# First token chunk as plain rows transposed on the matmul engine, loads reordered over two queues, gate logits in two parts

## The chip, the cores and the metric

The kernel runs on one core of one Trainium2 chip. The metric is device time in microseconds (us) of a whole execution. The profiler's span is about 1.5 us shorter than the timed run (293.3 against 294.8 us before the change).

Engine names in the profile: PE is the matmul engine, PEld its weight loads, DVE the vector engine, ACT the scalar engine, POOL the GpSimd engine, SP the sync engine. SPq and ACTq are the instruction streams of SP and ACT in so far as they issue DMA. "Full clock" and "half clock" are the clock that PE was granted, 1.00 and 0.50 in the tables. "The page" is the profile's summary page.

## The reference

One block of 2048 tokens, width 512, in bf16. Two branches are mixed by a per-token gate:

```python
g = sigmoid((x * gate_w).sum(-1))
# A: 4 segments of 512 tokens, 32 heads of 16; phi(t) = t + 1 where t > 0, else exp(t)
q, k, v = x @ wq, x @ wk, x @ wv
for s in range(4):
    a_dot = softmax(q_s k_s^T * scale + mask) v_s
    a_mem = phi(q_s) M / (phi(q_s) z + 1e-6)      # memory of earlier segments
    o_s   = sigmoid(beta) * a_mem + (1 - sigmoid(beta)) * a_dot
    M, z  = M + phi(k_s)^T v_s, z + sum(phi(k_s))
a = concat(o) @ wo
# B: feed-forward
b = (relu(x @ W_gate) * (x @ W_up)) @ W_down      # hidden width 1792
out = g * a + (1 - g) * b
```

A chunk of x is the 512 tokens of one segment: segment 0 needs only the first 512 tokens; the gate needs all tokens, but segment 0 only its own.

## The kernel before

The Python program is a list scheduler. It gives every operation an estimated duration, runs a model of the engines at build time, and emits one fixed instruction order for each engine, with semaphore waits between engines. So each engine runs in order: if the next instruction waits, all behind it wait. The model's DMA part is crude:

```python
# Sched.place(), for a DMA (cut): arrival times that the fixed order is built on
issued = start + occ
self.dma_free[e] = max(self.dma_free[e], issued) + op.nbytes / 150.0
op.end = self.dma_free[e] + 1500.0
```

Loads. x is wanted with features on partitions (`xT`), so it is loaded by 16 transposing DMAs on SP (4 for each chunk of 512 tokens), while ACT issues all weights:

```python
wload("wq", ...); wload("wk", ...)            # ACT queue; 512 KB each
...                                           # gate_w, beta, wv, gate/up weights, wo, wd: 7.6 MB in all
for c in range(NSEG):
    for kt in range(KT):
        xl.append(dma("sp", lambda e, c=c, kt=kt: e.dma_start_transpose(V.xT[:, kt, c * 512:(c + 1) * 512], A_x[...]),
                      1 << 17, occ=1280.0, writes=[f"xT{c}_{kt}"], name=f"ldx{c}_{kt}"))
```

PE is kept busy at the start with twelve matmuls on zeros (`warm`). The gate's logits are one group of 64 small matmuls that reads all of `xT` (`gmm`).

The keys for the memory update go through SP as well. ACT computes `ek = exp(k)`, DVE turns it into `phi(k)` in place, and SP transposes it into `phik`.

```python
acts.append(act(... V.ek[:, G, :] = exp(V.kT[:, G, :]) ..., writes=[f"ek{G}"], name=f"kexp{s}_{G}"))
sbs.append(dve(... V.ek[:, G, :] = min(V.ek, ttmp) ...,      writes=[f"ek{G}"], name=f"kphi{s}_{G}"))
sps.append(dma("sp", lambda e, G=G: e.dma_start_transpose(V.phik[:, :, G * 128:(G + 1) * 128], V.ek[:, G, :]), ...,
               reads=[f"ek{G}"], writes=[f"phik{G}"], name=f"kT2{s}_{G}"))
# memory update of segment s, first half: reads phik0, phik1
pes.append(pe(fn, mm(160, 8), reads=[f"phik{2 * hf}", f"phik{2 * hf + 1}"] + va(s), name=f"mu{s}_{hf}", ...))
```

Note two users of a key transpose: the memory update (`mu`) reads its result, and the *next* segment's `kexp` overwrites its source `ek`, so it must wait until the transpose has read it.

The softmax here doesn't subtract the row's maximum and nothing guards it: scores larger than these inputs give would overflow.

## Time and profile before

| | before |
|---|---|
| time, median of 3 | 294.81 us (294.5 to 295.98) |
| span of the profiled run | 293.3 us |
| PE busy | 269.9 us, 92% |
| first projection matmul | 17.81 us |
| first and last exponential of attention | 31.61 and 259.72 us |

PE is the bound. Its line on the page (busy us, share of the span, instructions):

```profile
PE 269.9 (92%) x2136; PEld 115.0 (39%) x2172; DVE 198.7 (68%) x391; ACT 184.2 (63%) x142; POOL 93.4 (32%) x150
...
```

Every matmul has one weight load, so 2136 matmuls against 2172 weight loads says that 36 matmul records are missing. A missing record can show as a gap of 0.16 to 0.24 us put down to "issue".

The table of windows (stretch in us, then its length, then busy us and instruction count of each engine; then the granted clock of PE, the mean busy share of the DMA engines, and GB/s):

```profile
core 0: us, PE busy (x) PEld busy (x) DVE busy (x) ACT busy (x) POOL busy (x), PEclk, DMA share, GB/s
0.00:5.00 5.00, 3.75 (x9) 1.34 (x10) 2.27 (x6) 0.00 (x0) 2.96 (x13) 1.00 0.61 155
5.00:10.00 5.00, 1.55 (x4) 0.30 (x2) 0.00 (x0) 0.00 (x0) 0.00 (x0) 1.00 1.03 137
10.00:20.00 10.00, 2.19 (x6) 0.84 (x7) 0.28 (x1) 1.09 (x1) 0.00 (x0) 0.50 1.10 336
20.00:35.00 15.00, 14.80 (x69) 5.96 (x69) 12.65 (x32) 6.34 (x10) 0.73 (x1) 0.88 1.17 310
35.00:40.00 5.00, 4.14 (x74) 2.37 (x74) 4.89 (x13) 4.18 (x4) 1.63 (x3) 1.00 0.55 79
40.00:50.00 10.00, 9.76 (x68) 4.26 (x67) 8.28 (x23) 7.55 (x9) 3.38 (x5) 0.83 0.19 39
```

The DMA engines are full from 5 to 35 us, but at 5 to 10 us they move only 137 GB/s. PE does nearly nothing until 18 us. The waits of the first 60 us say why (the engine, the tile and line that waited, what ended the wait; then us in all, times, longest), and the timeline shows the first real matmul:

```profile
PE psA L522 <- DMA xT<-in_A_x_dram: 11.3, 1, 11.3
```

```profile
1.25 5.30 PE L468 MATMUL psL<-rl 128*128 128x512 bf16 x12 [1.25 <-DVE rl L460]
...
17.81 1.87 PE L522 MATMUL psA<-xT,wq 128*128 128x512 bf16 x4 [11.26 <-DMA xT<-in_A_x_dram]
...
38.63 1.74 PE L486 MATMUL psA<-gwc,xT 128*128 128x1 bf16 x64 [0.70 <-DVE kp L538]
...
42.22 1.91 PE L522 MATMUL psA<-xT,wq 128*128 128x512 bf16 x4
```

The first two columns are start and length; the bracket is idle time of that engine just before, and what ended it. Line 522 is the projections; line 486 the gate. Wq was there at about 4.9 us; x came at 17.8. Four projection matmuls took 1.91 us at 42.22 us, and four such take 1.03 us elsewhere. After the gate PE ran at half clock for 3.4 us (40.77 to 44.18 us by the clock records of the trace).

### The profile page before, as it was taken

Reading aid. Unit: us, or ns where it says so; the run is one execution under the profiler, and the core shown is the slowest. Engines: PE = TensorE matmul, PEld = TensorE weight load, DVE = VectorE, ACT = ScalarE, POOL = GpSimd, SP = SyncE. Lnnn points to the kernel's source line nnn. Section 1 sums busy time; section 2 is a strip of 40 time slices with the busy share of each in tenths; the row PEclk is TensorE's granted clock in tenths of the full one; section 3 lists DMA queues with packets and bytes.
Section 4 is the critical chain, followed back from the end, with each engine's and each line's share of the span. In section 5 each row is a group of like instructions: output and inputs, shape, how many; then the busy total and the mean of one; then the engine's idle time right before and its main releaser. Section 6 shows DMA issues by size and latency. Waiting matters only on the chain.

```text
span 293.3 us, 5236 instructions
## 1 busy us (share of the span) xinstructions
PE 269.9 (92%) x2136; PEld 115.0 (39%) x2172; DVE 198.7 (68%) x391; ACT 184.2 (63%) x142; POOL 93.4 (32%) x150
## 2 busy tenths in 40 slices
PE   7059989799999999999999999999999999999895
PEld 2024344334444444434344434344344343344342
DVE  3027998999899989377889986458866354867100
ACT  0023678679785977768857967777677776763111
POOL 4000142553442533442424343343234334330000
PEclk9658979999999999999999999999999999999999
DMA  8999920001004131200001100100020000000011
GB/s 172 217 368 325 245 58 16 2 9 29 2 19 68 26 47 27 38 18 20 0 2 36 38 1 20 36 20 0 2 54 20 18 33 23 2 0 1 2 36 36
DMA packets 30791, 15.29 MB, mean 52 GB/s; under 512 B 22832, under 2 KB 30768, under 8 KB 30768
## 3 DMA queue, kind: packets, MB, share of 16 engines
q1 hardware_dynamic: 24064, 7.35, 12.9%
q10 hardware_dynamic: 6704, 7.61, 8.5%
q8 instruction: 17, 0.28, 0.4%
q14 instruction: 6, 0.05, 0.1%
HBM read 7.61 MB, written 2.10 MB: 33 GB/s over the span
## 4 chain that ended last, share of the span: by engine, by line
PE 85%; DVE 6%; DMA 4%; issue 2%; SPq 1%; ACT 0%; DVEq 0%; ACTq 0%
PE psA L685 32%; PE psA L716 17%; PE psA L522 10%; PE psL L615 8%; PE psA L640 6%; PE psA L708 5%; DMA xT<-in_A_x_dram 4%; PE psA L520 4%; SPq L437 1%; DVE vaug L546 1%; DVE kp L538 1%; PE psA L561 1%; PE psA L590 1%; DVE gexpT L494 1%; DVE qT L529 1%
## 5 line engine op out<-in xcount | busy, mean ns | idle before, releaser
L620 ACT ACTIVATE E<-psL 128x2048 bf16<-128x2048 f32 x80 | 150.1, 1876 | 44.3 <-PE psL L615 43.8
L623 POOL TENSOR_SCALAR_AFFINE_SELECT E<-E 128x512 bf16<-128x512 bf16 x128 | 83.9, 673 | 167.3 <-ACT E L620 166.1
L685 PE MATMUL psA<-xT,wg 128*128 128x512 bf16 x216 | 58.9, 380 | 1.8 <-DVE Tn L645 0.8
L685 PE MATMUL psA<-xT,wu 128*128 128x512 bf16 x217 | 57.3, 379 | 1.0 <-issue 1.0
L716 PE MATMUL psA<-wd,hT 128*128 128x512 bf16 x216 | 52.6, 380 | 0.8 <-issue 0.5
L696 DVE TENSOR_TENSOR hT<-psA,rl 128x512 bf16<-128x512 f32 x56 | 38.0, 679 | 8.3 <-PE psA L685 7.9
L645 DVE STREAM_TRANSPOSE Tn<-psA 128x512 f32<-128x512 f32 x32 | 21.5, 698 | 17.6 <-PE psA L640 17.4
L615 PE MATMUL psL<-qT,kp 32*128 32x384 bf16 (+3 forms) x512 | 31.7, 301 | 0.9 <-ACT E L620 0.8
L685 PEld LDWEIGHTS psA<-xT,wu 128*128 128x128 bf16 x224 | 20.9, 98 | 25.2 <-issue 1.4
L716 PEld LDWEIGHTS psA<-wd,hT 128*128 128x128 bf16 x224 | 20.4, 98 | 25.1 <-issue 3.4
L685 PEld LDWEIGHTS psA<-xT,wg 128*128 128x128 bf16 x224 | 19.6, 98 | 26.1 <-issue 4.3
L522 PE MATMUL psA<-xT,wq 128*128 128x512 bf16 x58 | 18.1, 432 | 11.8 <-DMA xT<-in_A_x_dram 11.3
L693 ACT ACTIVATE rl<-psA 128x512 bf16<-128x512 f32 x25 | 14.9, 596 | 16.8 <-PE psA L685 16.8
L529 DVE CAST qT<-psA 128x512 bf16<-128x512 f32 x16 | 11.0, 688 | 19.4 <-PE psA L522 19.3
L694 DVE TENSOR_SCALAR rl<-psA 128x512 bf16<-128x512 f32 x31 | 21.1, 682 | 4.1 <-PE psA L685 3.6
L615 PEld LDWEIGHTS psL<-qT,kp 32*128 32x128 bf16 x512 | 8.9, 92 | 32.5 <-ACT E L620 21.6
L640 PE MATMUL psA<-E,vaug 128*17 128x256 bf16 (+3 forms) x512 | 21.1, 300 | 0.0
L522 PE MATMUL psA<-xT,wk 128*128 128x512 bf16 x62 | 18.6, 418 | 0.3 <-issue 0.2
L721 ACT ACTIVATE osb<-psA,omg 128x512 bf16<-128x512 f32 x10 | 6.9, 687 | 17.3 <-PE psA L716 17.3
L708 PE MATMUL psA<-wo,oT 128*128 128x512 bf16 x62 | 16.2, 380 | 1.2 <-DVE hT L696 0.9
L520 PE MATMUL psA<-wv,xT 128*128 128x512 bf16 x61 | 15.0, 380 | 0.3 <-issue 0.2
L640 PEld LDWEIGHTS psA<-E,vaug 128*17 128x17 bf16 x512 | 10.5, 90 | 11.2 <-issue 4.2
(61 smaller groups left out, 201.7 us busy)
## 6 DMA issues: line engine op xcount, KB each, us to landing
out_dram<-osb SPq DMA_DIRECT2D x16, 128.0 KB, 1.7
wg<-in_B_W_gate_dram ACTq DMA_DIRECT2D x2, 896.0 KB, 14.1
wu<-in_B_W_up_dram ACTq DMA_DIRECT2D x2, 896.0 KB, 15.6
wd<-in_B_W_down_dram ACTq DMA_DIRECT2D x1, 1792.0 KB, 18.0
wq<-in_A_wq_dram ACTq DMA_DIRECT2D x1, 512.0 KB, 4.1
wk<-in_A_wk_dram ACTq DMA_DIRECT2D x1, 512.0 KB, 8.1
wv<-in_A_wv_dram ACTq DMA_DIRECT2D x1, 512.0 KB, 10.5
wo<-in_A_wo_dram ACTq DMA_DIRECT2D x1, 512.0 KB, 17.0
```

The costliest lines, as they stand in the source:

```text
L520: ins = e.matmul(A(ep)[:, :], lhsT=V.xT[:, kt, tok + col * 128:tok + (col + 1) * 128], rhs=w[:, kt, :], start=(kt == 0), stop=(kt == KT - 1))
L522: ins = e.matmul(A(ep)[:, :], lhsT=w[:, kt, col * 128:(col + 1) * 128], rhs=V.xT[:, kt, tok:tok + 512], start=(kt == 0), stop=(kt == KT - 1))
L615: ins = q.matmul(PL[:, jj, o:o + w], lhsT=V.kp[32 * jj:32 * jj + 32, kslot(s, n), 128 * j:128 * j + 128], rhs=V.qT[32 * jj:32 * jj + 32, q ...
L620: acts.append(act(lambda a, e=e: a.activation(V.E[:, e, :, :], PL[:, :, :], ACT.Exp, scale=SCALE), t_act(2048), reads=[f"bankL{b}" for b i ...
L623: pools.append(pool(lambda g, ap=ap: g.affine_select(out=ap, in_=ap, compare_op=ALU.is_ge, fill=0.0, base=0, pattern=[[0, 4], [1, 128]], c ...
L640: ins = q.matmul(A(ep)[32 * jj:32 * jj + 17, c:512], lhsT=V.vaug[:, s % 2, j, 8 * G + 2 * jj + p, :], rhs=V.E[:, e, jj, o:o + w], start=(j ...
L645: ds.append(dve(lambda e, p=p, ep=eps[p]: e.transpose(V.Tn[:, p, :], A(ep)[:, :]), t_dve(512), writes=[f"Tn{p}"], name=f"tr{s}_{G}_{p}", e ...
L685: ins = e.matmul(A(ep)[:, :], lhsT=w[:, kt, f * 128:(f + 1) * 128], rhs=V.xT[:, kt, c * 512:(c + 1) * 512], start=(kt == 0), stop=(kt == K ...
L694: ("dve", lambda e, ep=eg, r=r: e.tensor_scalar(V.rl[:, r, :], A(ep)[:, :], 0.0, None, ALU.max), t_dve(512))],
L696: evs.append(dve(lambda e, ep=eu, r=r, hs=hs: e.tensor_tensor(V.hT[:, hs, :], A(ep)[:, :], V.rl[:, r, :], ALU.mult), t_dve(512), reads=[f" ...
L708: ins = e.matmul(A(ep)[:, :], lhsT=V.oT[:, o0 + G, i * 128:(i + 1) * 128], rhs=V.wo[:, G, :], start=(G == 0), stop=False)
L716: ins = e.matmul(A(ep)[:, :], lhsT=V.hT[:, slots[f], i * 128:(i + 1) * 128], rhs=V.wd[:, f, :], start=False, stop=(f == NF - 1))
```

## The change

The intent is to start earlier. The first chunk comes as plain rows (4 x 128 KB, split over SP and ACT) into a part of `hT` that is not in use yet; 16 matmuls with an identity transpose it into PSUM, and four copies put it into `xT`. wq, wk, wv follow in halves on both queues; all later loads are on SP in order of first use, with the x of chunks 2 and 3 last. The gate is split into a part for chunk 0 and a part for the rest. The cost model of the scheduler changes too (one shared DMA rate of 330 bytes/ns and 1800 ns to land).

```diff
-            self.dma_free[e] = max(self.dma_free[e], issued) + op.nbytes / 150.0
-            op.end = self.dma_free[e] + 1500.0
+            self.dma_busy = max(self.dma_busy, issued) + op.nbytes / 330.0
+            op.end = self.dma_busy + 1800.0
...
+    for i, eng in enumerate(("sp", "act", "sp", "act")):
+        load(eng, [f"hT{i}"], V.hT[:, i, :], x0[:, i, :], 1 << 17)
+    for nm, w, src in (("wq", V.wq, A_wq), ("wk", V.wk, A_wk), ("wv", V.wv, A_wv)):
+        load("sp", [nm + "a"], w[:, 0:2, :], r[:, 0:2, :], 1 << 18)
+        load("act", [nm + "b"], w[:, 2:4, :], r[:, 2:4, :], 1 << 18)
+    load("sp", ["braw"], ...)          # beta
+    load_gu(0)                         # first half of gate and up weights
+    lsp.append(... ld_gw ...)          # gate_w
+    load_x(1)                          # 4 transposing loads
+    load_gu(1)
+    load("sp", ["wo"], ...)
+    load("sp", ["wd"], ...)
+    for c in range(2, NSEG):
+        load_x(c)                      # 8 transposing loads
...
-        for i in range(12):            # warm-up matmuls
+    xps, xcs = [warm(WARM, 0)], []     # WARM = 5
+    for i in range(4):
+        def fx(e, i=i):
+            for kt in range(KT):
+                ins = e.matmul(PL[:, i, kt * 128:(kt + 1) * 128], lhsT=V.hT[:, i, kt * 128:(kt + 1) * 128], rhs=V.ident[:], start=True, stop=True)
...
-    gp = pe(f_gmm, NT * KT * 30.0, reads=[x for c in range(NSEG) for x in xt(c)] + ["gwc"], name="gmm", ep=ep_g, role="w")
+    for part, (t0, t1) in enumerate(((0, 4), (4, NT))):
+        gq["pe"].append(pe(f_gmm, (t1 - t0) * KT * 26.0, reads=[x for c in range(t0 // 4, t1 // 4) for x in xt(c)] + ["gwc"], name=f"gmm{part}", ...))
...
-  "oa{s}_{i}" reads [f"hT{x}" for x in slots]
+  "oa{s}_{i}" reads [f"hT{x}" for x in (slots if s < NSEG - 1 else slots[:NF - 4])]
```

Cuts are marked by "..."; left out are the small gate copies (now on DVE or ACT) and a few duration estimates.

More of the change, by code (lines that the diff above doesn't have):

```diff
@@ L16 @@
 SWITCH = 100.0
+WARM = 5
 def mm(n, k=1):
@@ L95, in __init__ @@
         self.res = {}
-        self.now = {e: 0.0 for e in self.ENGS}
+        self.now = {e: 800.0 for e in self.ENGS}
         self.mode = "f"
@@ L100, in __init__ @@
         self.dma_end = {}
-        self.dma_free = {e: 0.0 for e in self.ENGS}
+        self.dma_busy = 0.0
         self.prog = {e: [] for e in self.ENGS}
@@ L353, in plan @@
         ("gexp", [128, NT], F32), ("omg", [128, NT], F32), ("gexpT", [128, NT * 4], F32), ("c2g", [128, NT, 32], F32),
-        ("rden", [128, 32], F32), ("rdg", [128, 32], F32), ("rdm", [128, 128], F32), ("pm8", [128, 8], F32), ("pm", [128, 2], F32),
+        ("rden", [128, 32], F32), ("rdg", [128, 32], F32), ("rdm", [128, 128], F32), ("pm8", [128, 8], F32), ("pm", [128, 2], F32), ("ident", [128, 128], BF16),
     ]
@@ L407, in xt, with load, load_gu, load_x @@
         return [f"xT{c}_{kt}" for kt in range(KT)]
-    loads = []
-    def wload(name, dst, src, nbytes):
-        loads.append(dma("act", lambda e, dst=dst, src=src: e.dma_start(dst, src), nbytes, writes=[name], name="ld" + name))
-    wload("wq", V.wq[:], A_wq.rearrange("(kt p) n -> p kt n", p=128), 1 << 19)
-    wload("wk", V.wk[:], A_wk.rearrange("(kt p) n -> p kt n", p=128), 1 << 19)
-    with nc.allow_non_contiguous_dma(reason="one column of gate weights"):
-        gsrc = gate_w.rearrange("(kt p) -> p kt", p=128)
+    lact, lsp = [], []
+    def load(eng, names, dst, src, nbytes, occ=460.0):
+        (lact if eng == "act" else lsp).append(dma(eng, lambda e, dst=dst, src=src: e.dma_start(dst, src), nbytes, occ=occ, writes=names, name="ld" + names[0]))
+    x0 = A_x[0, 0:512, :].rearrange("(i p) d -> p i d", p=128)
+    for i, eng in enumerate(("sp", "act", "sp", "act")):
+        load(eng, [f"hT{i}"], V.hT[:, i, :], x0[:, i, :], 1 << 17)
+    for nm, w, src in (("wq", V.wq, A_wq), ("wk", V.wk, A_wk), ("wv", V.wv, A_wv)):
+        r = src.rearrange("(kt p) n -> p kt n", p=128)
+        load("sp", [nm + "a"], w[:, 0:2, :], r[:, 0:2, :], 1 << 18)
+        load("act", [nm + "b"], w[:, 2:4, :], r[:, 2:4, :], 1 << 18)
+    wgr = W_g.rearrange("(kt p) n -> p kt n", p=128)
+    wur = W_u.rearrange("(kt p) n -> p kt n", p=128)
+    half = (NF // 2) * 128
+    hs_ = ((0, half), (half, NF * 128))
+    def load_gu(h):
+        a, b = hs_[h]
+        load("sp", [f"wg{h}"], V.wg[:, :, a:b], wgr[:, :, a:b], 512 * 2 * (b - a))
+        load("sp", [f"wu{h}"], V.wu[:, :, a:b], wur[:, :, a:b], 512 * 2 * (b - a))
+    def load_x(c):
+        for kt in range(KT):
+            lsp.append(dma("sp", lambda e, c=c, kt=kt: e.dma_start_transpose(V.xT[:, kt, c * 512:(c + 1) * 512], A_x[0, c * 512:(c + 1) * 512, kt * 128:(kt + 1) * 128]),
+                           1 << 17, occ=1280.0, writes=[f"xT{c}_{kt}"], name=f"ldx{c}_{kt}"))
+    load("sp", ["braw"], V.braw[:], A_beta.partition_broadcast(128), 8192)
+    load_gu(0)
+    gsrc = gate_w.rearrange("(kt p) -> p kt", p=128)
     def ld_gw(e):
@@ L420, in ld_gw @@
             return e.dma_start(V.gwc[:], gsrc)
-    loads.append(dma("act", ld_gw, 60000, writes=["gwc"], name="ldgw"))
-    wload("braw", V.braw[:], A_beta.partition_broadcast(128), 8192)
-    wload("wv", V.wv[:], A_wv.rearrange("(kt p) n -> p kt n", p=128), 1 << 19)
-    wgr = W_g.rearrange("(kt p) n -> p kt n", p=128)
-    wur = W_u.rearrange("(kt p) n -> p kt n", p=128)
-    half = (NF // 2) * 128
-    for h, (a, b) in enumerate(((0, half), (half, NF * 128))):
-        wload(f"wg{h}", V.wg[:, :, a:b], wgr[:, :, a:b], 512 * 2 * (b - a))
-        wload(f"wu{h}", V.wu[:, :, a:b], wur[:, :, a:b], 512 * 2 * (b - a))
-    wload("wo", V.wo[:], A_wo.rearrange("(g p) n -> p g n", p=128), 1 << 19)
-    wload("wd", V.wd[:], W_d.rearrange("(f p) n -> p f n", p=128), NF * 128 * 1024)
-    sc.queue(0, loads)
-    xl = []
-    for c in range(NSEG):
-        for kt in range(KT):
-            xl.append(dma("sp", lambda e, c=c, kt=kt: e.dma_start_transpose(V.xT[:, kt, c * 512:(c + 1) * 512], A_x[0, c * 512:(c + 1) * 512, kt * 128:(kt + 1) * 128]),
-                          1 << 17, occ=1280.0, writes=[f"xT{c}_{kt}"], name=f"ldx{c}_{kt}"))
-    sc.queue(0, xl)
+    lsp.append(dma("sp", ld_gw, 60000, writes=["gwc"], name="ldgw"))
+    load_x(1)
+    load_gu(1)
+    load("sp", ["wo"], V.wo[:], A_wo.rearrange("(g p) n -> p g n", p=128), 1 << 19)
+    load("sp", ["wd"], V.wd[:], W_d.rearrange("(f p) n -> p f n", p=128), NF * 128 * 1024)
+    for c in range(2, NSEG):
+        load_x(c)
+    sc.queue(0, lact)
+    sc.queue(0, lsp)
     st = []
+    st.append(pool(lambda e: e.memset(V.ident[:], 1.0), 150, writes=["ident"], name="id0"))
+    st.append(pool(lambda e: e.affine_select(out=V.ident[:], in_=V.ident[:], compare_op=ALU.is_equal, fill=0.0, base=0, pattern=[[1, 128]], channel_multiplier=-1),
+                   260, reads=["ident"], writes=["ident"], name="id1"))
     st.append(pool(lambda e: e.memset(V.pm8[:], 1.0), 150, writes=["pm8"], name="pm8a"))
@@ L464, in program, with warm, fn @@
     sc.queue(0, ds)
-    def f_warm(e):
-        for i in range(12):
-            ins = e.matmul(PL[:, 0, :], lhsT=V.rl[:, 0, 0:128], rhs=V.rl[:, 0, :], start=True, stop=True)
-        return ins
-    sc.queue(0, [pe(f_warm, 5000, reads=["rl0"], writes=["bankL0"], name="warm")])
+    def warm(n, k):
+        def fn(e):
+            for i in range(n):
+                ins = e.matmul(PA[0][:, :], lhsT=V.rl[:, 0, 0:128], rhs=V.rl[:, 0, :], start=True, stop=True)
+            return ins
+        return pe(fn, n * 427, reads=["rl0"], writes=["init0"], name=f"warm{k}")
+    xps, xcs = [warm(WARM, 0)], []
+    for i in range(4):
+        def fx(e, i=i):
+            for kt in range(KT):
+                ins = e.matmul(PL[:, i, kt * 128:(kt + 1) * 128], lhsT=V.hT[:, i, kt * 128:(kt + 1) * 128], rhs=V.ident[:], start=True, stop=True)
+            return ins
+        xps.append(pe(fx, 430, reads=[f"hT{i}", "ident"], writes=[f"bankL{i}"], name=f"xt{i}"))
+        dst = V.xT[:, :, i * 128:(i + 1) * 128]
+        srcp = PL[:, i, :].rearrange("q (k t) -> q k t", k=KT)
+        xcs.append(sc.add(Op([("dve", lambda e, d=dst, s_=srcp: e.tensor_copy(d, s_), t_dve(512)),
+                              ("act", lambda e, d=dst, s_=srcp: e.activation(d, s_, ACT.Copy), t_act(512))],
+                             reads=[f"bankL{i}"], writes=[f"xT0_{i}"], name=f"xc{i}")))
+    sc.queue(0, xps)
+    sc.queue(0, xcs)
     cst = [act(lambda e: e.activation(V.eb[:], V.braw[:], ACT.Exp), 300, reads=["braw"], writes=["eb"], name="eb")]
@@ L479, in program @@
     sc.queue(1, [t for t in cst if t.eng == "dve"])
-    ep_g = Epoch()
-    def f_gmm(e):
-        for t in range(NT):
-            for kt in range(KT):
-                ins = e.matmul(A(ep_g)[:, t:t + 1], lhsT=V.xT[:, kt, t * 128:(t + 1) * 128], rhs=V.gwc[:, kt:kt + 1], start=(kt == 0), stop=(kt == KT - 1))
-        return ins
-    gp = pe(f_gmm, NT * KT * 30.0, reads=[x for c in range(NSEG) for x in xt(c)] + ["gwc"], name="gmm", ep=ep_g, role="w")
-    ga = act(lambda e: e.activation(V.gexp[:, :], A(ep_g)[:, 0:NT], ACT.Exp), 190, writes=["gexp"], name="gexp", ep=ep_g, role="r")
@@ L490, in program @@
-    gd = [dve(lambda e: e.tensor_scalar(V.omg[:], V.gexp[:], 1.0, None, ALU.add), 180, reads=["gexp"], writes=["omg1"], name="omg1"),
-          dve(lambda e: e.reciprocal(V.omg[:], V.omg[:]), 250, reads=["omg1"], writes=["omg"], name="omg")]
-    for a in range(4):
-        for jj in range(4):
-            gd.append(dve(lambda e, a=a, jj=jj: e.tensor_copy(V.gexpT[32 * jj:32 * jj + 32, :].rearrange("q (t a) -> q t a", a=4)[:, :, a], V.gexp[32 * a:32 * a + 32, :]),
-                          150, reads=["gexp"], writes=[f"gexpT{a}{jj}"], name="gexpT"))
@@ L496, in program, with f_gmm @@
-    gd.append(dve(lambda e: e.tensor_tensor(V.c2g[:], V.eb[:, :].unsqueeze(1).to_broadcast([128, NT, 32]), V.gexp[:, :].unsqueeze(2).to_broadcast([128, NT, 32]), ALU.mult),
-                  t_dve(NT * 32), reads=["eb", "gexp"], writes=["c2g"], name="c2g"))
-    gexpT_r = [f"gexpT{a}{jj}" for a in range(4) for jj in range(4)]
-    sc.queue(3, [gp])
-    sc.queue(1, [ga])
-    sc.queue(1, gd)
+    gexpT_r = {}
+    gq = {"pe": [], "act": [], "dve": [], "flex": []}
+    for part, (t0, t1) in enumerate(((0, 4), (4, NT))):
+        ep_g = Epoch()
+        def f_gmm(e, t0=t0, t1=t1, ep_g=ep_g):
+            for t in range(t0, t1):
+                for kt in range(KT):
+                    ins = e.matmul(A(ep_g)[:, t - t0:t - t0 + 1], lhsT=V.xT[:, kt, t * 128:(t + 1) * 128], rhs=V.gwc[:, kt:kt + 1], start=(kt == 0), stop=(kt == KT - 1))
+            return ins
+        gq["pe"].append(pe(f_gmm, (t1 - t0) * KT * 26.0, reads=[x for c in range(t0 // 4, t1 // 4) for x in xt(c)] + ["gwc"], name=f"gmm{part}", ep=ep_g, role="w"))
+        gx = V.gexp[:, t0:t1]
+        gq["act"].append(act(lambda e, t0=t0, t1=t1, gx=gx, ep_g=ep_g: e.activation(gx, A(ep_g)[:, 0:t1 - t0], ACT.Exp), 190, writes=[f"gexp{part}"], name="gexp", ep=ep_g, role="r"))
+        om = V.omg[:, t0:t1]
+        gq["dve"].append(dve(lambda e, om=om, gx=gx: e.tensor_scalar(om, gx, 1.0, None, ALU.add), 180, reads=[f"gexp{part}"], writes=[f"omg1{part}"], name="omg1"))
+        gq["dve"].append(dve(lambda e, om=om: e.reciprocal(om, om), 250, reads=[f"omg1{part}"], writes=[f"omg{part}"], name="omg"))
+        gexpT_r[part] = []
+        for a in range(4):
+            for jj in range(4):
+                dst = V.gexpT[32 * jj:32 * jj + 32, :].rearrange("q (t a) -> q t a", a=4)[:, t0:t1, a]
+                gq["flex"].append(sc.add(Op([("dve", lambda e, a=a, dst=dst, t0=t0, t1=t1: e.tensor_copy(dst, V.gexp[32 * a:32 * a + 32, t0:t1]), 150),
+                                             ("act", lambda e, a=a, dst=dst, t0=t0, t1=t1: e.activation(dst, V.gexp[32 * a:32 * a + 32, t0:t1], ACT.Copy), 215)],
+                                            reads=[f"gexp{part}"], writes=[f"gexpT{part}_{a}{jj}"], name="gexpT")))
+                gexpT_r[part].append(f"gexpT{part}_{a}{jj}")
+        if part:
+            gq["dve"].append(dve(lambda e, t0=t0: e.tensor_tensor(V.c2g[:, t0:, :], V.eb[:, :].unsqueeze(1).to_broadcast([128, NT - t0, 32]), V.gexp[:, t0:].unsqueeze(2).to_broadcast([128, NT - t0, 32]), ALU.mult),
+                                 t_dve((NT - t0) * 32), reads=["eb", f"gexp{part}"], writes=["c2g"], name="c2g"))
@@ L503, in kslot @@
+    sc.queue(2, gq["pe"][:1])
+    sc.queue(4, gq["pe"][1:])
+    sc.queue(1, gq["act"])
+    sc.queue(1, gq["dve"])
+    sc.queue(2, gq["flex"])
     def kslot(s, n):
@@ L523, in fn @@
                     return ins
-                pes.append(pe(fn, mm(512, 2), reads=[wname] + xt(s), name=f"{name}{s}_{col}", ep=ep, role="w2" if k0 else "w"))
+                pes.append(pe(fn, mm(512, 2), reads=[wname + ("b" if k0 else "a")] + xt(s), name=f"{name}{s}_{col}", ep=ep, role="w2" if k0 else "w"))
             return ep
@@ L537, in proj @@
                 ks = kslot(s, 2 * G + p)
-                evs.append(dve(lambda e, G=G, p=p, ks=ks: e.tensor_scalar(V.kp[:, ks, :], V.kT[:, G, :], V.pm[:, p:p + 1], None, ALU.mult), t_dve(512, 4), reads=[f"kT{G}", "pm"], writes=[f"kp{ks}"], name=f"kmask{s}_{G}_{p}"))
+                evs.append(dve(lambda e, G=G, p=p, ks=ks: e.tensor_scalar(V.kp[:, ks, :], V.kT[:, G, :], V.pm[:, p:p + 1], None, ALU.mult), 417, reads=[f"kT{G}", "pm"], writes=[f"kp{ks}"], name=f"kmask{s}_{G}_{p}"))
             if s < NSEG - 1:
@@ L649, in flush @@
             ds.append(dve(lambda e: e.reciprocal(rv, Tv[:, :, :, 16]), 345, reads=["Tn0", "Tn1"], writes=["rden"], name=f"rden{s}_{G}"))
-            ds.append(dve(lambda e: e.tensor_tensor(gv, rv, V.gexpT[:, 16 * s:16 * s + 16].unsqueeze(1).to_broadcast([128, 2, 16]), ALU.mult), 180, reads=["rden"] + gexpT_r, writes=["rdg"], name=f"rdg{s}_{G}"))
+            ds.append(dve(lambda e: e.tensor_tensor(gv, rv, V.gexpT[:, 16 * s:16 * s + 16].unsqueeze(1).to_broadcast([128, 2, 16]), ALU.mult), 264, reads=["rden"] + gexpT_r[min(s, 1)], writes=["rdg"], name=f"rdg{s}_{G}"))
             av = V.adT[:, :].rearrange("q (c p e) -> q p c e", p=2, e=16)
-            ds.append(dve(lambda e: e.tensor_tensor(av, Tv[:, :, :, 0:16], gv.unsqueeze(3).to_broadcast([128, 2, 16, 16]), ALU.mult), t_dve(512), reads=["Tn0", "Tn1", "rdg"], writes=["adT"], name=f"ad{s}_{G}"))
+            ds.append(dve(lambda e: e.tensor_tensor(av, Tv[:, :, :, 0:16], gv.unsqueeze(3).to_broadcast([128, 2, 16, 16]), ALU.mult), 806, reads=["Tn0", "Tn1", "rdg"], writes=["adT"], name=f"ad{s}_{G}"))
             os_ = (s % 2) * 4 + G
@@ L709, in fa @@
                 return ins
-            pes.append(pe(fa, mm(512, 4), reads=[f"oT{o0 + G}" for G in range(4)] + ["wo", "wd"] + [f"hT{x}" for x in slots], name=f"oa{s}_{i}", ep=ep, role="w"))
+            pes.append(pe(fa, mm(512, 4), reads=[f"oT{o0 + G}" for G in range(4)] + ["wo", "wd"] + [f"hT{x}" for x in (slots if s < NSEG - 1 else slots[:NF - 4])], name=f"oa{s}_{i}", ep=ep, role="w"))
             for f0 in range(0, NF, 2):
@@ L721, in outp @@
                                   ("act", lambda e, ep=ep, r=r, t=t: e.activation(V.osb[:, r, :], A(ep)[:, :], ACT.Copy, scale=V.omg[:, t:t + 1]), t_act(512, True, 1))],
-                                 reads=["omg"], writes=[f"osb{r}"], name=f"fin{s}_{i}", ep=ep, role="r")))
+                                 reads=[f"omg{min(s, 1)}"], writes=[f"osb{r}"], name=f"fin{s}_{i}", ep=ep, role="r")))
             sps.append(dma("sp", lambda e, r=r, t=t: e.dma_start(out[0, t * 128:(t + 1) * 128, :], V.osb[:, r, :]), 1 << 17, reads=[f"osb{r}"], writes=[f"out{t}"], name=f"st{t}"))
```

## The prediction

> **What bounds the kernel now.** The matmul engine. The page gives PE 92% busy; the table of windows gives 39.4 of 40 us at 60-100 and 98.4 of 100 at 100-200. DVE (68%) and ACT (63%) have slack. What PE loses, it loses at the start. The timeline shows warm-up matmuls from 1.25 to 6.55 us, then nothing until 17.81 us; the waits put this idle 11.3 us down to the DMA of xT. That is the first chunk of x, four transposing loads (128 KB each) that share the DMA engines with 7.6 MB of weights (DMA share 1.0 or more from 5 to 35 us, but only 155 and 137 GB/s in the first two 5 us windows). wq, a plain 512 KB load, landed at about 4.9 us: the weights were there, x was not.
>
> **What the change does.** It loads the first chunk as rows (512 KB, plain) ahead of wq, wk, wv, over both queues; 16 matmuls with an identity transpose it, and 4 copies (DVE or ACT, 0.6 to 0.7 us each by the trace's evictions of this shape) fill xT. The other 12 transposing loads go behind the weights needed earlier. The Trainium skill (DMA: Bandwidth & Descriptors, "Issuing engines are not separate DMA queues") says a second queue saves only issue time; I expect the gain from order and kind of load.
>
> New start, estimated: rows land at 3.5-4 us (issue at 0.8; wq took 4.1 us for four times one load's bytes), transposes and copies about 2 us, wq (1 MB in all by then, at 300 GB/s or so, the rate in 10-30 us) at about 6 us. First projection at 6.5 us in place of 17.8: **-11.3 us**. All of it is on the critical path: PE is 98% busy after 60 us, and fixed work starts earlier. The projections will again run at half clock for some us (now 17.8 to 23.7); Trainium skill, TensorE: Matmul & The Clock Gate, "The HAM clock gate": idle PE is throttled; the trace agrees (0.50 in 15-20). I count no gain there.
>
> Smaller terms: the last segment's output no longer waits for its last four hidden tiles (0.94 us PE gap at 273-274 us): -0.7. Twice as many small gate copies (0.16 us each, off the path): 0. Moving 64 gate matmuls (1.74 us in all): 0.
>
> Given back: the PE order is fixed at build, and the x of chunks 2 and 3 comes last. DMA work is about 25 us for the weights and, worked out from the queues' shares, 1.1 us per transpose, so about 40 us; the last x lands at 40-45 us, now about 38. The second gate matmul, which reads all of it, or chunk 1's projections (x at 20-23 us) can stall PE by 1-3 us. After 60 us nothing changes.
>
> **Prediction:** 294.8 - 11.3 - 0.7 + about 1 = **283.8 us**, 8 in 10 between 280.0 and 288.0. Faster by over 2%: 0.92; within 2%: 0.07; slower: 0.01.
>
> **What would show it.** First projection matmul at 6-7.5 us; the 11 us wait on xT gone; first exponential near 20 us in place of 31.6; the last exponential and the end about 11 us earlier; PE busy only about 3 us lower (fewer warm-up matmuls), so its share rises to 94-95%; PE gaps with the releaser DMA xT between 20 and 50 us of 3 us at most.
>
> **What would make it wrong.** Rows land late because weights crowd the same engines; the gate's second part stalls PE for 5 us or more, and the clock drops with it; key transposes to phik queue behind all loads on SP and hold up the memory update; the projection phase turns out DVE bound. The other way: early PE gaps and the half clock near 41-45 us vanish, for 2-3 us more.

## The result

| | before | after |
|---|---|---|
| time, median of 4 each | 294.99 us | 287.49 us (287.23 to 287.63) |
| ratio | | 0.9741 (95%: 0.9714 to 0.9767) |
| span | 293.3 us | 285.8 us |
| PE busy | 269.9 us, 92% | 267.7 us, 94% |
| first projection | 17.81 us | 6.74 us |
| first, last exponential | 31.61, 259.72 us | 22.56, 257.09 us |

A ratio is the mean time of one kernel's fast runs over that of the other's of the same rounds, so it is not quite the ratio of the medians. The kernel is 7.5 us faster. The start moved by 11.1 us, as forecast. So 3.6 us were given back. Here is the page's PE line and the same windows as above:

```profile
PE 267.7 (94%) x2145; PEld 116.0 (41%) x2181; DVE 197.3 (69%) x383; ACT 194.5 (68%) x173; POOL 92.1 (32%) x152
...
```

```profile
core 0: us, PE busy (x) PEld busy (x) DVE busy (x) ACT busy (x) POOL busy (x), PEclk, DMA share, GB/s
0.00:5.00 5.00, 3.16 (x15) 1.78 (x16) 2.27 (x6) 1.66 (x2) 3.40 (x15) 1.00 0.61 170
5.00:10.00 5.00, 4.12 (x17) 1.68 (x15) 2.08 (x3) 0.82 (x2) 0.00 (x0) 1.00 0.89 299
10.00:20.00 10.00, 9.95 (x59) 4.70 (x59) 8.65 (x23) 5.03 (x17) 0.00 (x0) 1.00 1.05 259
20.00:35.00 15.00, 14.68 (x92) 5.93 (x92) 12.98 (x30) 13.04 (x17) 3.90 (x6) 1.00 1.21 292
35.00:40.00 5.00, 0.58 (x3) 0.09 (x1) 2.37 (x5) 0.68 (x1) 1.22 (x2) 0.80 0.52 111
40.00:50.00 10.00, 7.82 (x99) 4.42 (x104) 3.53 (x13) 5.33 (x9) 1.39 (x2) 0.59 0.14 28
```

At 5 to 20 us PE is at work where it stood before. But at 35 to 40 us PE (0.58 of 5 us) and ACT (0.68) nearly stand, DVE works half of the time (2.37), and the clock falls to 0.59 in the window after it. The waits and the timeline show one gap:

```profile
PE psA L602 <- issue: 6.3, 1, 6.3
...
ACT ek L581 <- DMA phik<-ek: 5.5, 2, 4.8
```

```profile
3.95 1.91 PE L491 MATMUL psL<-ident,hT 128*128 128x128 bf16 x16
...
6.74 1.86 PE L563 MATMUL psA<-xT,wq 128*128 128x512 bf16 x4 [0.88 <-DVE xT L496]
...
34.55 1.03 PE L563 MATMUL psA<-xT,wq 128*128 128x512 bf16 x4
41.85 1.07 PE L602 MATMUL psA<-vaug,phik 128*128 128x136 bf16 x8 [6.26 <-issue]
42.70 1.47 PE L519 MATMUL psA<-gwc,xT 128*128 128x1 bf16 x48
...
46.32 1.91 PE L726 MATMUL psA<-xT,wg 128*128 128x512 bf16 x4
```

Line 602 is the first half of the memory update of segment 0. "Issue" means that the view found no releaser; it is not an answer. The instruction's inputs are `vaug`, long there, and `phik`. SP's own stream, and the chain of waits around 38 us, name it:

```profile
6.21 10.32 SPq L433 DMA_TRANSPOSE xT<-in_A_x_dram  x4
...
19.10 18.84 SPq L433 DMA_TRANSPOSE xT<-in_A_x_dram  x8
...
37.98 23.55 SPq L584 DMA_TRANSPOSE phik<-ek  x5
```

```profile
37.94 0.04 issue
37.98 2.50 DMA phik<-ek
40.49 1.36 issue
41.85 1.07 PE psA L602 x8
```

SP issues in order. The key transposes stand behind the eight transposing loads of chunks 2 and 3, and these took 18.84 us to issue. The first of the eight alone took 9.05 us (the chain of waits, 19.10 to 28.15), each of the last five 1.26 us. The keys that the memory update's first half needs were ready before: DVE wrote these two from 27.15 and 29.17 us, and was done with them by 29.6 us:

```profile
27.15 0.86 DVE L583 TENSOR_TENSOR ek<-ek,ttmp 128x512 bf16<-128x512 bf16 x1
...
29.17 0.41 DVE L583 TENSOR_TENSOR ek<-ek,ttmp 128x512 bf16<-128x512 bf16 x1
```

ACT stood in the same stretch, because its next exponential overwrites `ek` that the transpose had not read.

The sum, from the page and the timeline. Idle PE time after the first projection is the span less PE busy less the idle time before: before the change 293.3 - 269.9 - (1.25 + 11.26) = 10.9 us; after it 285.8 - 267.7 - (1.84 + 0.88) = 15.4 us. (36 records are missing in both, 2136 against 2172 and 2145 against 2181, so the difference stands.) So the span moved by -11.1 (start) + 4.5 (idle) - 0.9 (busy time past the start, 264.6 to 263.7), which is the -7.5 measured; it must be, since start, idle and busy time make up the span.

One caution about the start: 6.74 us is the early end. In the profiles of later runs whose loads begin in the same order (experiments 1 to 3), the first projection came at 6.74 to 8.30 us, the late ones waiting for wq.

### The profile page after: what moved, and what is told of

Same layout as the page of the kernel before. It is cut to its first block, busy times and chain, and to the rows that moved or that the text cites. A ratio compares the mean times of both kernels' runs of the same rounds, so it can differ in the third digit from the quotient of the medians.

```text
span 285.8 us, 5289 instructions
## 1 busy us (share of the span) xinstructions
PE 267.7 (94%) x2145; PEld 116.0 (41%) x2181; DVE 197.3 (69%) x383; ACT 194.5 (68%) x173; POOL 92.1 (32%) x152
## 4 chain that ended last, share of the span: by engine, by line
PE 78%; SPq 13%; issue 3%; ACT 3%; DVE 2%; DMA 1%; ACTq 0%; DVEq 0%
PE psA L726 30%; PE psA L757 16%; SPq L433 10%; PE psL L656 8%; PE psA L681 7%; PE psA L563 5%; PE psA L749 5%; PE psA L561 4%; SPq L413 2%; ACT E L661 2%; PE psA L602 1%; PE psA L631 1%; DMA phik<-ek 1%; DVE hT L737 1%; PE psA L519 0%
## 5 line engine op out<-in xcount | busy, mean ns | idle before, releaser
L664 POOL TENSOR_SCALAR_AFFINE_SELECT E<-E 128x512 bf16<-128x512 bf16 x128 | 82.3, 661 | 159.3 <-ACT E L661 159.3
L726 PE MATMUL psA<-xT,wu 128*128 128x512 bf16 x215 | 58.6, 384 | 1.1 <-DVE omg L526 0.3
L734 ACT ACTIVATE rl<-psA 128x512 bf16<-128x512 f32 x33 | 19.6, 595 | 15.8 <-PE psA L726 14.9
L563 PE MATMUL psA<-xT,wq 128*128 128x512 bf16 x60 | 16.9, 401 | 1.4 <-DVE xT L496 0.9
L735 DVE TENSOR_SCALAR rl<-psA 128x512 bf16<-128x512 f32 x23 | 15.8, 686 | 2.9 <-PE psA L726 2.3
L563 PE MATMUL psA<-xT,wk 128*128 128x512 bf16 x61 | 17.2, 396 | 0.4 <-DVE ttmp L582 0.2
L581 ACT ACTIVATE ek<-kT 128x512 bf16<-128x512 bf16 x12 | 7.5, 627 | 9.6 <-DMA phik<-ek 5.5
```

The costliest lines, as they stand in the source:

```text
L563: ins = e.matmul(A(ep)[:, :], lhsT=w[:, kt, col * 128:(col + 1) * 128], rhs=V.xT[:, kt, tok:tok + 512], start=(kt == 0), stop=(kt == KT - 1))
L664: pools.append(pool(lambda g, ap=ap: g.affine_select(out=ap, in_=ap, compare_op=ALU.is_ge, fill=0.0, base=0, pattern=[[0, 4], [1, 128]], c ...
L726: ins = e.matmul(A(ep)[:, :], lhsT=w[:, kt, f * 128:(f + 1) * 128], rhs=V.xT[:, kt, c * 512:(c + 1) * 512], start=(kt == 0), stop=(kt == K ...
```

## The experiments

All kernels gave the reference's result. "Ratio" is to the kernel before, of the same rounds; "after" has 0.9741. Ratios of different calls are compared across each other; the medians of the kernel before were 295.31, 296.01 and 295.42 us in the three calls, and 294.99 us in the call of the result.

### 1. Which wait holds PE: the keys, or the gate behind them?

**The first two key transposes ahead of chunks 2 and 3.** Only SP's instruction list is rearranged after scheduling.

```diff
  SP:  ... wo, wd,
+      phik0, phik1 (segment 0),
       xT chunk 2 (4), xT chunk 3 (4),
-      phik0, phik1, phik2, phik3, ...
+      phik2, phik3, ...
```

> After the change PE starts at 6.74 us as forecast, but stands 6.3 us at 35.6-41.9 us, before the first memory-update matmul, whose key transposes (phik) sit on SP behind all x loads. This run moves only the first two phik transposes ahead of the x loads of chunks 2 and 3; PE, ACT, DVE and POOL keep their order. Theory A (the phik transposes alone hold PE): the stall goes, with its half clock (about 2.3 us), so 279 us. Theory B (the next instruction in PE's fixed order, the gate's second part, waits for the last x, which lands at about 40.5 us and now 2.5 us later): the stall moves to the gate matmul, PE idle about 5-6 us there, 286-289 us.

Measured: 287.32 us, ratio 0.9732 (0.97 to 0.9765). Nothing gained. The PE timeline of this run:

```profile
34.73 0.64 PE L602 MATMUL psA<-vaug,phik 128*128 128x136 bf16 x8
42.38 1.42 PE L519 MATMUL psA<-gwc,xT 128*128 128x1 bf16 x48 [7.01 <-DMA xT<-in_A_x_dram]
```

The memory update no longer waits. PE then stands 7.01 us at the next instruction, the gate's second part, for the last x. Theory A fell, B held.

**The gate's second part late.** The gate's second part (`gmm1`) is created after attention of segment 0 and made to depend on its second output group.

```diff
-    gmm1 reads xT1..xT3, gwc            (scheduled as soon as the model has x)
+    gmm1 reads xT1..xT3, gwc, oT1
```

> Only the gate's second part is put late (after attention's second group of segment 0); loads and SP order up to the phik transposes stay. Theory A and B: the wait for phik stays, PE idle about 6 us before the first memory-update matmul, 286.5-288.5 us. Theory C (the late x behind the gate is the cause, the phik wait only happens to be in front): PE loses nothing any more, 279-281 us.

Measured: 289.06 us, ratio 0.9803 (0.9774 to 0.9831). The 6.3 us in front of the memory update stay:

```profile
42.62 1.07 PE L603 MATMUL psA<-vaug,phik 128*128 128x136 bf16 x8 [6.30 <-issue]
```

Theory C, that the gate alone is the cause, fell. It came out half a microsecond above the expected range. In its profile the first projection came 0.7 us later than after the change (7.43 us, waiting for wq); whether that is the reason is not shown.

**Both together.**

> Both: two phik transposes ahead of x chunks 2 and 3 on SP, and the gate's second part late. Theory B: both waits gone, no PE gap over 1 us between 20 and 60 us, clock stays full there, 278-281 us. Theory A: no better than the first run of this set (279). If neither stall is the cause of the shortfall: 286-288 us.

Measured: 287.61 us, ratio 0.9747 (0.9711 to 0.9782). Both theories expected 278 to 281: both missed. The number lies in the third range, "if neither stall is the cause"; by the number alone one would have dropped the queue as the cause. The trace shows a third user of the same queue:

```profile
42.59 14.05 SPq L585 DMA_TRANSPOSE phik<-ek  x2
...
45.16 0.63 ACT L582 ACTIVATE ek<-kT 128x512 bf16<-128x512 bf16 x1 [5.74 <-DMA phik<-ek]
...
47.61 0.61 PE L657 MATMUL psL<-qT,kp 32*128 32x256 bf16 x8 [5.02 <-ACT E L662]
```

PE ran on to 42.6 us. Then ACT stood 5.74 us for the *third* key transpose, still behind the x loads, because it had to overwrite its source; so no attention exponential ran, and PE stood 5.02 us for it. One queue, three places to stand. This led to the next theory: the cause is the position of the whole group of key transposes, and each user in turn shows it.

**All four key transposes before or between the late x loads, gate late.**

```diff
  SP:  ... wo, wd,
+      phik0, phik1, phik2,
       xT chunk 2 (4),
+      phik3,
       xT chunk 3 (4), ...
```

> The stall has moved twice: from the memory update to the gate (first run), and with both cleared to ACT, which stands 5.7 us because its next exponential overwrites a key tile that the third phik transpose has not read yet; PE then stands 5.0 us. Theory D: one cause, the key transposes behind the x loads in SP's single order; every user of them in turn stands. This run puts all four key transposes of segment 0 before or between the x loads of chunks 2 and 3 and keeps the gate late: no PE gap over 1.5 us between 20 and 60 us, clock full, 278.5-281 us. Rival: the early lead is limited by something else (ACT or DVE work between 20 and 60 us), and whatever is cleared comes back: 285.5-288 us.

Measured: 280.5 us, ratio 0.9476 (0.944 to 0.9512). The profile of this run, where PE works from 20 to 60 us without a gap and at full clock:

```profile
35.00:40.00 5.00, 5.00 (x44) 2.19 (x46) 4.98 (x11) 4.74 (x7) 2.62 (x4) 1.00 0.32 71
40.00:50.00 10.00, 10.00 (x89) 4.18 (x78) 8.67 (x18) 7.74 (x5) 3.24 (x5) 1.00 0.23 45
```

The theory held, and the rival (ACT or DVE work limits the lead, 285.5 to 288 us) fell. This run differs from "both together" only in the place of the third and fourth key transposes. From 0.9741 to 0.9476 is 7.8 us of 295. Not every such wait is gone: up to 79.99 us PE stands 1.39 us for a key transpose of the next segment, and half clock follows (81.30 to 84.72 us).

### 2. The same cure without moving a load

If the queue's order can stay and only the waiting instructions move, the cause is better named as a fixed order built on too early arrivals. Here one rule changes in the scheduler's model: a transposing DMA (of x, of the keys, of the memory's output) holds SP until the loads before it have drained. The loads on SP keep their order; the order on the other engines is worked out anew.

```diff
+            if op.name.startswith(("ldx", "kT2", "aT")):
+                issued = max(start, self.dma_busy) + occ
+                occ = issued - start
             self.dma_busy = max(self.dma_busy, issued) + op.nbytes / 330.0
```

> The loads stay in their order; only the scheduler's model learns that a transposing load holds SP until the loads before it have drained, so that it places the memory update, the gate's second part and the exponentials that wait for phik later. If the cause is the fixed order built on too early arrivals: PE gap over 1.5 us between 20 and 60 us gone, 279-283 us. If order can't help because work that is free of those waits is missing: 286-289 us.

Measured: 280.24 us, ratio 0.9445 (0.941 to 0.948), the lowest, though its interval overlaps that of the run before. The key transposes still start only at 38.98 us, one microsecond later than after the change, yet PE is busy 39.98 of the 40 us from 20 to 60 us:

```profile
sum 40.00, PE 39.98 PEld 16.67 DVE 35.13 ACT 34.80 POOL 13.57; mean PE 10.00 PEld 4.17 DVE 8.78 ACT 8.70 POOL 3.39
```

There was enough free work to put in front of the waits; the model had not known that it should.

### 3. What the half clock costs

Twenty-seven unneeded matmuls are put where PE stands; nothing else moves.

```diff
  PE:  wait psA bank free (DVE)
+      27 x matmul(psA bank, wq, wq)     # overwritten by the next instruction
       wait phik0, phik1
       memory update, first half
```

> The kernel after the change with 27 unneeded matmuls (about 5.8 us at full clock) put where PE stands before the first memory-update matmul, after the wait for its PSUM bank and before the wait for phik. Nothing else changes. If the idle time is what drops the clock, the half clock at 44-49 us goes: about 2 us faster, 285.0-286.0 us, clock 1.00 in 40-50 us in place of 0.59. If the clock drops for another reason, no change (287.5) or slower.

Measured: 286.06 us, ratio 0.9677 (0.9646 to 0.9708), so 1.9 us better than after the change, and the clock is 1.00 at 40 to 50 us. PE's timeline of this run (26 of the 27 were recorded):

```profile
35.62 5.99 PE L831 MATMUL psA<-wq 128*128 128x512 bf16 x26
43.23 0.63 PE L604 MATMUL psA<-vaug,phik 128*128 128x136 bf16 x8 [1.61 <-DMA phik<-ek]
...
46.17 1.03 PE L728 MATMUL psA<-xT,wg 128*128 128x512 bf16 x4
```

The keys came somewhat later in this run than in the profile of after, and still the time fell. Four matmuls take 1.03 us some 3 us after the stall where they took 1.91 us. This agrees with the Trainium skill, "TensorE: Matmul & The Clock Gate", "The HAM clock gate", which has the clock drop to half after an idle window of about 3.4 us: 6.26 us of standing dropped it, the 1.61 us left here did not. So the stall of 6.3 us cost, by estimate, about 8.2 us (6.3 + 1.9); experiment 1 got back 7.8, which is near. A part of the 1.9 may be the start: in this profile the first projections already ran at full clock, and the first matmul with wv came 0.4 us earlier than after the change (15.15 against 15.58 us).

### 4. Is it the plain loads ahead on the same queue?

The second half of the gate and up weights, wo and wd are issued on ACT, after the first chunk's copies.

```diff
-    SP:  ..., xT chunk 1, wg1, wu1, wo, wd, xT chunks 2 and 3, phik...
+    SP:  ..., xT chunks 1, 2 and 3, phik...
+    ACT: ..., copies of xT chunk 0, wg1, wu1, wo, wd, ...
```

> The second half of the gate and up weights, wo and wd (4.1 MB) are issued on ACT after the first chunk is in place; SP has only x and keys after the first weights. If SP's two long issues (5.9 and 9.1 us for the first transposing load behind plain loads) come from plain loads ahead on the same queue: the second long issue disappears, the last x is issued before 33 us (37.9 after the change), the key transposes start when their data is there, stall under 2 us, 279-283 us. If they come from the bytes outstanding on any queue: the last x is issued as late as now and the stall stays, 286-289 us.

Measured: 288.63 us, ratio 0.9749 (0.9711 to 0.9787). The lines of SP and PE:

```profile
6.38 30.49 SPq L433 DMA_TRANSPOSE xT<-in_A_x_dram  x12
...
21.64 0.58 PE L521 MATMUL psA<-gwc,xT 128*128 128x1 bf16 x16 [4.50 <-DMA gwc<-in_gate_w_dram]
```

My first hypothesis fell: with the weights on another queue the twelve transposing loads still took 30.49 us to issue, to 36.87 us (37.94 after the change); the first of them alone took 9.87 us. The long issue before chunk 2 went, but the others became longer. This fits the other half of the expectation, that the bytes in flight slow SP wherever they were issued. Experiment 1 fits it too: with two key transposes put first, the eight loads of chunks 2 and 3 were issued from 30.16 us, 11 us later than after the change, and took 10.40 us in place of 18.84. The Trainium skill, "DMA: Bandwidth & Descriptors", "Issuing engines are not separate DMA queues", says that all such queues run on the same 16 DMA engines; the trace agrees. The earlier weights also crowd the small ones: `gate_w`, 1 KB, landed 15.8 us after issue (10.2 us after the change), and PE stood 4.5 us for it. That other half was wrong in one point: the stall for the keys did not stay, because PE, held up by `gate_w` and the half clock after it, reached the memory update only at 43.11 us (PE is busy 15.00 of the 15 us from 35 to 50 us). The time, 288.63 us, lies in the range expected for a stall that stays, but for another stall.

### 5. What the parts of the change are worth

**Order alone**: the new queues and order, but chunk 0 by four transposing loads at the head of SP.

```diff
-    load(eng, [f"hT{i}"], V.hT[:, i, :], x0[:, i, :], 1 << 17)      # and the identity matmuls and copies
+    lsp.append(dma("sp", ... e.dma_start_transpose(V.xT[:, kt, 0:512], A_x[0, 0:512, ...]), ..., name=f"ldx0_{kt}"))
```

> The new load order and queues, but the first chunk by four transposing loads at the head of SP, as before, and no identity matmuls. If order is the larger part of the gain: projections start at 9-10 us in place of 6.7, 289-291.5 us. If the plain rows are: start after 12 us, 293 us or more.

Measured: 292.51 us, ratio 0.9892 (0.9848 to 0.9937).

```profile
9.85 1.87 PE L551 MATMUL psA<-xT,wq 128*128 128x512 bf16 x4 [5.69 <-DMA wq<-in_A_wq_dram]
```

The start is at 9.85 us, as expected, and waits there for wq, which is issued behind the four transposing loads; the time is 1 us above the range, with a stall of 6.8 us at the memory update.

**Rows alone**: the kernel before, with chunk 0 as rows on SP, identity matmuls and copies (and five warm-up matmuls in place of twelve); all else as before, the gate in one part.

```diff
-    for c in range(NSEG):          # 16 transposing loads on SP
+    for i in range(4): xl.append(dma("sp", ... e.dma_start(V.hT[:, i, :], x0[:, i, :]) ...))
+    for c in range(1, NSEG):       # 12 transposing loads on SP
```

> The kernel before with only the first chunk's four loads replaced by plain rows, identity matmuls and copies (on DVE); weights on ACT and the order of loads as before, and the gate's logits in one part. The projections start near 7 us, about 11 us earlier. But the fixed order now puts the whole gate, which reads all of x, after the first projection of chunk 1, at about 20-22 us, and the last x lands at about 33-38 us. If waits in PE's fixed order give the early start back: PE stands 12-16 us at the gate and the time is 293-299 us. If the rows are worth their lead by themselves: 284-287 us.

Measured: 295.17 us, ratio 0.9986 (0.9952 to 1.0021): worth nothing by itself.

```profile
9.86 0.60 PE L483 MATMUL psL<-ident,hT 128*128 128x128 bf16 x4 [2.08 <-DMA hT<-in_A_x_dram]
11.34 1.86 PE L543 MATMUL psA<-xT,wq 128*128 128x512 bf16 x4 [0.88 <-DVE xT L488]
...
34.55 1.85 PE L507 MATMUL psA<-gwc,xT 128*128 128x1 bf16 x64 [6.46 <-DMA xT<-in_A_x_dram]
```

Two things were off in what I expected. The rows came one by one, the last for 9.86 us, most likely because the weights on the other queue were not held back (not tested): the start was 11.34 us, not 7. And the stall at the one-part gate was 6.46 us, not 12 to 16. PE also stood 2.26 us before 20.58 us, for DVE. Yet the main point held: PE's early start ran into the gate and was given back. Rows and order need each other (9.85 and 11.34 us alone, 6.74 together). That the split gate is part of the cure is argued from this stall; no run isolates it.

**Warm-up matmuls**: after the change, without the five.

> The kernel after the change without its five warm-up matmuls; all else in place. If they shorten the half-clock stretch of the first projections (6.7 to about 11.2 us now): full clock comes up to 2 us later and the time is 0.5-1 us longer. If they do nothing: same within 0.4 us.

Measured: 287.67 us, ratio 0.9727 (0.9702 to 0.9751). They do nothing that this can show. In these two profiles the spacing of the matmuls changes to full clock at about 11.4 us without them and at about 10.7 us with them (worked out from the group that holds the change: 1.46 us from 10.19 to 11.65 here, where four matmuls take 1.71 at half and 0.86 at full clock); that would be some 0.3 us of work, too little to see in the time. One profile of each can't settle it: in three other runs with the same five matmuls at the start (first two keys, all four keys, and the 27 unneeded matmuls) full clock came at 5.85 to 6.45 us, before the first projection. The timeline without them:

```profile
8.48 1.91 PE L563 MATMUL psA<-xT,wk 128*128 128x512 bf16 x4
10.19 1.63 PE L563 MATMUL psA<-xT,wq 128*128 128x512 bf16 x4
11.65 1.03 PE L563 MATMUL psA<-xT,wk 128*128 128x512 bf16 x4
```

**Tail**: the kernel before, with only the last segment's output released ten hidden tiles in.

> The kernel before with only the last segment's output released ten hidden tiles in, not all fourteen. Forecast in the prediction: 0.7 us shorter (the 0.94 us gap at 273-274 us goes). If the gap only moves to another wait: no change within 0.3 us.

Measured: 295.87 us, ratio 0.9999 (0.997 to 1.0028). The interval contains the -0.7 us that I forecast, so the time alone decides nothing. The trace speaks against it: the scheduler put the output matmuls earlier, and a gap of 0.86 us at 278.76 us for a hidden tile took the place of 0.94 us at 274.22 us. In the profile of after the change there is no such gap in front of the outputs, so there the term may exist; no run here isolates it.

**Scheduling alone**: the kernel before, with one duration in the model set to the traced one.

```diff
-    occ=1280.0   # transposing x load
+    occ=2150.0
```

> The kernel before, with one number of the scheduler's model changed: a transposing x load holds SP for 2150 ns (34.5 us for 16 in the trace) in place of 1280. Loads are the same. If the kernel before also lost time to a gate placed before its x was there: the gap before the gate at 37-38.6 us and the half clock at 41-45 us go, 2 to 4 us faster, 291-293 us. If not: 294.5-295.5 us.

Measured: 295.43 us, ratio 1.0003 (0.9969 to 1.0037). The expectation missed. The gap before the gate and the half clock at 41 to 45 us went, but the gate moved to 54.12 us and PE ran at half clock again at 57.9 to 60 us, and the 60 to 100 us window has PE busy only 38.1 of 40. So in the kernel before, this one number is not enough; what would be enough there was not searched for.

## Why the prediction was right, and which term was mis-sized

The number held (287.5 within 280 to 288, forecast 283.8), but near the upper edge. Point by point:

- *Start at 6.5 us, -11.3 us.* Right: 6.74 us, -11.1 us, and the wait on xT is gone. The reason given (order and kind of load, not queues) is half shown: order alone gives 9.85 us, rows alone 11.34 us, both 6.74 us. Which queue carries the weights was not tried with everything else equal.
- *"All of it is on the critical path."* Right for PE's total, but only while PE has work that waits for nothing.
- *No gain or loss at the first half clock.* Right: about 4 us from the first projection to full clock, worked out from the spacing of its matmuls (the group at 10.11 us), and about 5.9 us before the change. So by estimate about 1 us less was lost there (half of the 1.9 us), where the sum had 0; in some other profiles full clock came earlier still (see "Warm-up matmuls").
- *Tail, -0.7 us.* Not shown; alone it moved the gap (0.86 us for 0.94 us).
- *"Given back ... can stall PE by 1-3 us", about 1 in the sum.* **This is the term that was mis-sized.** The stall was 6.3 us and took 1.9 us of half clock with it, together 8.2 us; the idle time past the start rose by 4.5 us net, because the kernel before had early losses of its own that went. What the sum left out is a path: it saw only the landing of the last x, not that everything behind the x loads in SP's order is held while they are issued (18.84 us for eight). I named the last x with the gate, or chunk 1's projections, as the likely place. The prediction's list of risks also had the actual first place, the key transposes behind all loads on SP, without a size. The last x arrives as forecast, soon after 40 us; that this would hold three users in turn (memory update, gate, ACT's overwrite) I had not seen.
- *First exponential near 20 us, last exponential about 11 us earlier.* Wrong: 22.56 us, and only 2.6 us earlier (257.09 against 259.72). The end moved by 7.5 us, more than the last exponential, so this was a poor proxy for the end. Likely the stall held attention but not the feed-forward work done before it; that was not tested.
- *PE share 94 to 95%, busy about 3 us lower.* Right: 94%, 2.2 us lower.
- *PE gaps with the releaser DMA xT between 20 and 50 us of 3 us at most.* Literally true and useless: the gap was 6.3 us, with another releaser.

With the stall cured the gain is 5.2 to 5.6% (0.9476, 0.9445), 15 to 16 us, which is more than the 12 us of my sum without the give-back. The kernel before lost time at 36 to 45 us as well (a gap at the gate, then half clock), and these two runs have no gap and no half clock there. That this is the whole of the extra 3 to 4 us is argued, not shown.

## What to carry to other kernels

When a start is moved forward, list every consumer that is placed by an arrival time, and check each arrival against its queue: the order on the queue, not the need, decides when a load goes out, and an in-order engine stops at the first that is late. When removing one wait changes nothing, look for the next wait on the same queue before giving up the theory. The build-time model needs the measured holding time of each kind of load on its queue; here three lines of it were worth about 3% (0.9741 to 0.9445).

## What the Trainium skill lacked or had wrong

- "DMA: Bandwidth & Descriptors": it has no figure for how long a transposing load holds its issuing queue under other traffic. In these runs 1.26 us with little else in flight, 9.05 us for the first one behind 4096 KB of plain loads, and 30.49 us for twelve with those weights on the other queue. The prediction gave issue time no term in its sum; here it held the keys back.
- The same page, "Anatomy of one DMA": it gives a fixed cost of about 2 us for a DMA (measured on the GpSimd path), and no figure for a small load under traffic. The 1 KB load of `gate_w`, which the program asks for as single 2-byte values, landed after 10.2 us, and after 15.8 us with more weights in flight; what the small pieces add to that is not shown.
- "TensorE: Matmul & The Clock Gate", "The HAM clock gate": it puts the rise to full clock at about 4 us of sustained matmuls, give or take 0.5. By the clock records of these traces the spread is wider. Before the change it came 5.4 us after the first warm-up matmul (1.25 to 6.64 us, just as the twelve ended; it was lost again at 10.05 us, while PE stood), and 5.9 us after the first projection (17.81 to 23.70). After the change it came about 4 us after the first projection (10.69 us), in the run with the gate late 3.0 us after the first warm-up matmul (1.84 to 4.87 us). In each trace the recorded changes lie whole multiples of 3.41 us apart (before: 6.64, 10.05, 23.70, 40.77 and 44.18 us), so it matters where on this grid the first matmul falls, and that differs from run to run.
- No page says whether matmuls of one column keep the clock up. Before the change the clock dropped at 40.77 us with no idle gap over 0.70 us in the 3.4 us before; 1.74 us of these were the gate's 64 one-column matmuls. With 48 of them at 51.54 us, in the run of experiment 2, it did not drop.
- "TensorE: Matmul & The Clock Gate" also warns that the clock's trace records can be unreliable. What misled here was the view of them: it reads 1.00 until the first recorded change (10.69 us after the change), while four 512-wide matmuls take 1.9 us there, the half-clock time.
